# Turning q with DMA transposes of 16-bit halves, and taking the words apart on ScalarE, in a fused attention and feed-forward kernel

## The chip, the cores and the metric

The kernel runs on one core of one Trainium2 chip. The metric is the device time in microseconds (us) of that core for one launch. Every kernel was timed several times beside the kernel before on the same chip. A ratio below is the mean time of one kernel's fast runs over the mean of the other's fast runs of the same rounds, so it is not quite the ratio of the medians quoted beside it.

The names of the profile: PE is TensorE (matmuls), PEld its weight loads, ACT ScalarE, DVE VectorE, POOL GpSimd, SP SyncE. SyncE issues most DMAs; SPq marks its queue.

## The reference, cut to what matters

```python
kv  = einsum('bhsd,bhse->bhde', k, v)     # batch 8, heads 8, seq 576, head_dim 64
out = einsum('bhsd,bhde->bhse', q, kv)
out = out / sqrt(mean(out*out, -1) + 1e-6) * g_norm
x   = out.transpose(0, 2, 1, 3).reshape(4608, 512)
result = (((x @ w1) * (x @ w2)) @ w3) @ w_out
```

In this kernel the matmuls of `q @ kv` take q with head_dim on the partitions, while it arrives with tokens there. It has to be turned: 128x128 blocks of fp32.

## The kernel before

w3 and w_out are folded into one matrix first. Then the work goes by batches: the gates `(x @ w1) * (x @ w2)` of one batch in four parts p (Winograd-style, seven products each), its projection, and in between, in small pieces, the attention of the next batch. TensorE's list is in the program's order; the lists of ScalarE, VectorE and SyncE are ordered by a scheduler when the kernel is built.

```python
def q_t(r):                                   # q of one pair of heads
    q_sb = loaded["q", b, r]
    qt_ps = bank(ps_at, "at").rearrange("p (e i t) -> p e i t", e=2, i=2)
    for e in range(2):
        for i in range(2):
            nc.tensor.transpose(qt_ps[:, e, i, :], q_sb[:, e, i * P:(i + 1) * P], ident)
    qT[r] = work.tile([P, 2, 2, P], FP32, name="qT")
    nc.scalar.copy(qT[r], qt_ps)
...
# winograd: the start of the seven products of a gate
r1 = product("a11", "b11"); p1 = keep("p1", r1)      # keep = ScalarE copy PSUM -> SBUF
r2 = product("s1", "t1");   p5 = keep("p5", r2)
product("s2", "t2", r1);    u2 = keep("u2", r1)      # adds into bank r1: waits for the copy p1
between()                                            # a piece of attention
product("s4", "b22", r2)                             # waits for the copy p5
done("c12", r2, u2)
product("s3", "t3", r1);    u3 = keep("u3", r1)      # waits for the copy u2
...
```

q is called in program order as `begin_q(0, 1)` in piece 0 of the next batch and `begin_q(2, 3)` in piece 2; their users, the products of attention, are in pieces 1 and 5.

Of the kernel before, what the change touches and what calls it, by code (L numbers as in the profile page):

```python
# [10 lines left out]

FP32 = mybir.dt.float32
U32 = mybir.dt.uint32
I64 = mybir.dt.int64
AF = mybir.ActivationFunctionType
ALU = mybir.AluOpType
# [4 lines left out]
def kernel(  # L21
# [32 lines left out]
    nc = tc.nc  # L54
    PSUM = bass.MemoryType.PSUM
    P = 128
# [4 lines left out]
    NP = H // 2  # L61
# [11 lines left out]
    work = ctx.enter_context(tc.tile_pool(name="work", bufs=2))  # L73
    ps_mm = ctx.enter_context(tc.tile_pool(name="ps_mm", bufs=5, space=PSUM))
    ps_at = ctx.enter_context(tc.tile_pool(name="ps_at", bufs=3, space=PSUM))
# [5 lines left out]
    def bank(pool, tag):  # L81
        return pool.tile([P, 512], FP32, name=tag, tag=tag)


    loaded = {}
    q_left = {}
# [43 lines left out]
    def conversion(n, dst, raw, cols=slice(0, 1024)):  # L130

        dst, raw = (t if len(t.shape) == 3 else t[:, cols] for t in (dst, raw))
        if raw.dtype == FP32:
            yield
            nc.vector.tensor_copy(out=dst, in_=raw)
            return
        words = raw.bitcast(U32).rearrange("p (n w) -> p n w", w=2)
        lo, hi = words[:, :, 0], words[:, :, 1]

        low = ab[n % 2][:, NF // 2:].rearrange("p a i t -> p (a i t)")[:, cols]  # L140
        low_bits = low.bitcast(U32)
        if len(dst.shape) == 3:
# [3 lines left out]
            )  # L146
        dst_bits = dst.bitcast(U32)
        nc.scalar.activation(low, lo, AF.Copy, scale=2.0 ** -51, bias=2.0)
# [85 lines left out]
    def all_of(steps):  # L234
        for _ in steps:
            pass


    ident = const.tile([P, P], FP32, name="ident")
# [13 lines left out]
    def keep_warm(n):  # L253

        t = bank(ps_mm, "mm")
        for _ in range(n):
            nc.tensor.matmul(t[:, 0:P], lhsT=ident, rhs=ident, start=True, stop=True)


    def attention(b):  # L260
        kv_b = kv_sb[b % 3]
        qT = {}
# [28 lines left out]
        def q_t(r):  # L291
# [6 lines that stand above are left out]
            qT[r] = work.tile([P, 2, 2, P], FP32, name="qT")  # L298
            nc.scalar.copy(qT[r], qt_ps)

        st = {}

        def q_t_left():
            st["qT"] = work.tile([P, NP, P], FP32, name="qT_left", bufs=1)
            qt_ps = bank(ps_at, "at").rearrange("p (r t) -> p r t", r=NP)
            for r in range(NP):
                nc.tensor.transpose(qt_ps[:, r, :], q_left[b // 2][:, 2 * r:2 * r + 2, :], ident)  # L307
            nc.scalar.copy(st["qT"], qt_ps)

        def norm(o_ps, dsts):  # L310

# [85 lines left out]
        def load_ahead(names, r):  # L397

            if r + 2 < NP:
                load_pair(names, b, r + 2)  # L400
            elif b + 1 < B:
                load_pair(names, b + 1, r + 2 - NP)
                if r + 1 == NP and "k" in names:
                    load_kv_left(b + 1)

        def begin_kv(*rs):
            kv(rs)
            for r in rs:
                load_ahead("kv", r)

        def begin_q(*rs):
            for r in rs:
                q_t(r)
                load_ahead("q", r)

        def begin(r):
            begin_kv(r)
            begin_q(r)

        def finish(h):  # L420
            all_of(product(h))

        return SimpleNamespace(**{f.__name__: f for f in (
            start, begin_kv, begin_q, begin, product, finish, turn, q_t_left, product_left, turn_left,
        )})

    batches = {}

    def batch(b):
        if b not in batches:  # L430
            batches[b] = attention(b)
        return batches[b]

    def steps(b):


        a = batch(b)
        a.start()
        more = b + 1 < B
        fs = [[] for _ in range(8)]  # L440
        if b == 1:
            fs[0].append((a.begin_kv, 0, 1))
        fs[0].append((a.begin_q, 0, 1))
        fs[1] += [(a.begin_kv, 2, 3), (a.finish, 0)]
        fs[2].append((a.begin_q, 2, 3))
        fs[3] += [(a.turn, 0), (a.turn, 1)]
        if more:
            fs[5].append((batch(b + 1).begin_kv, 0, 1))
        fs[5].append((a.finish, 1))
        fs[7] += [(a.turn, 2), (a.turn, 3)]  # L450
        if b % 2:
            fs[2].insert(0, (a.q_t_left,))
            fs[6].append((a.product_left,))
            fs[7].append((a.turn_left,))
            if more:
                fs[7].append((load_q_left, b + 1))
        elif more:
            fs[0].append((load_q_left, b + 1))
        return iter([lambda s=s: [f(*args) for f, *args in s] for s in fs])
# [95 lines left out]
    def run(*step_lists):  # L555

        for steps in zip(*step_lists):
            for step in steps:
                step()
# [50 lines left out]
    def sum_ab(p):  # L610
        aa[p] = {f"a{i + 1}{j + 1}": ab[j][:, p, i, :] for i in range(2) for j in range(2)}
        return sums(aa[p], free["ab", p])
# [10 lines left out]
    def gates(T, p, between, ready=lambda name: None):  # L623
        def done(name, one, two):
            multiply(name, one, two)
            ready(name)

        def multiply(name, one, two):

            dst = ab[int(name[1]) - 1][:, p, int(name[2]) - 1, :]  # L630
            if two is None:
                c = late_pool.tile([P, N], FP32, name="c21")
                nc.scalar.copy(c, one[:, 0, :])  # L633
                nc.vector.tensor_mul(dst, c, one[:, 1, :])
                return
            c = late_pool.tile([P, 2, N], FP32, name="c")
            nc.vector.tensor_add(c, one, two)  # L637
            nc.vector.tensor_mul(dst, c[:, 0, :], c[:, 1, :])  # L638

        winograd(  # L640
            lambda name, w, c: wa[p][name][:, w, c, :],
            lambda name, c: xb[T][name][:, c, :],
            NP // 2, done, between,
        )
# [31 lines left out]
    def stage_tile():  # L676
        return late_pool.tile([P, 3, 2, P], FP32, name="stage")
# [43 lines left out]
    def sum_inner(n, between=lambda: None):  # L721

        s1, s2, s4 = ab_sums
        x = [ab[0][:, :, 0], s1, s2, s4, ab[0][:, :, 1], ab[1][:, :, 0], ab[1][:, :, 1]][n]
        a11, a12, a21, a22 = (
            x[:, 2 * j:2 * j + 2, i * P:(i + 1) * P] for i in range(2) for j in range(2)
        )
        s1, s2, s4 = inner_sums[n % 3]
        nc.vector.tensor_add(s1, a21, a22)
        nc.vector.tensor_sub(s2, s1, a11)  # L730
        nc.vector.tensor_sub(s4, a12, s2)
        between()
        nc.vector.tensor_sub(a21, a11, a21)
        inner[n] = [a11, a12, a22, s1, s2, s4, a21]
# [145 lines left out]
    with tc.manual_schedule(  # L880
# [6 lines left out]
        for e in range(2):  # L887
            nc.scalar.dma_start(
                out=g_row[:, e * D:(e + 1) * D], in_=g_norm.rearrange("(o d) -> o d", o=1)
# [75 lines left out]
    groups = [*range(B - 1), B, B - 1]  # L965
    for n, T in enumerate(groups):
        pieces = steps(T + 1) if n + 2 < NG else iter([])

        def between():
            next(pieces, lambda: None)()  # L970

        for p in range(NF):
            if T and p + 1 == NF:
                sum_1, sum_2, sum_4, sum_3 = sum_ab(p)
                following = {
                    "c12": [], "c22": [sum_1],
                    "c11": [
                        lambda: sum_inner(0, lambda: all_of(f() for f in (sum_2, sum_3))),
                        lambda: sum_inner(1),
                    ],  # L980
                    "c21": [sum_4],
                }
                gates(T, p, between, lambda name: all_of(f() for f in following[name]))
                continue
            gates(T, p, between if T or p else lambda: None)
            if T == 0:
                if p + 1 < NF:
                    run(sum_w(p + 1))
                for _ in range(2):
                    if len(converted) < len(todo):  # L990
                        begin_next()
                        end_next()
                if p + 1 == NF:
                    allocate_projection()
                    run(*(f(i) for i in range(NF) for f in (sum_ab, combine_w3o)))
            else:
                run(sum_ab(p))
        last = n + 1 == NG
        if T:
            project_twice(T, last, [] if last else combine_x(groups[n + 1]))  # L1000
            continue
        project(T, between)
        run(combine_x(1))
        prepare_b()
        for _ in range(3):
            load_b()
        stage = stage_tile()
        inner_sums.append([stage[:, i] for i in range(3)])
# [30 lines left out]
```

## Time and profile before

| | before |
|---|---|
| time | 794.4 us (794.05 to 794.71) |
| TensorE busy | 784.4 of 792.2 us, 99% |
| ScalarE busy | 282.2 us, 36% |
| mean granted TensorE clock | 0.999 |
| turning q on TensorE | 128 + 16 transposes, 17.2 + 2.4 us of busy time |

The first rows say that TensorE sets the time, and that the change takes work off the engine that counts. The records of these transposes overlap (one lasts 275 ns, and 128 of them make 17.2 us, 134 ns each). The clock row matters later: the clock column of the kernel before is 1.00 until behind its last matmul (0:785 and 785:790 us). The lines themselves are in the prediction.

### The profile page before, as it was taken

How to read it: one execution, taken by the hardware profiler on the slowest of the kernel's cores; microseconds unless marked ns; L12 is line 12 of the kernel's file. 1: busy time of each engine (PE TensorE's matmuls, PEld its weight loads, DVE VectorE, ACT ScalarE, POOL GpSimd, SP SyncE). 2: the span in 40 equal slices, each digit the busy share in tenths (PEclk: the TensorE clock that was granted, in tenths of full speed). 3: DMA queues.
4: the chain of work that ended last, by engine and by line, in shares of the span. 5: the costliest groups of instructions: out<-in, count | busy, mean ns of one | idle time of the engine just before them, and what ended most of it. 6: DMA issues, size and time to landing. Idle time of an engine off the chain costs nothing.

```text
span 792.2 us, 14634 instructions
## 1 busy us (share of the span) xinstructions
PE 784.4 (99%) x6003; PEld 683.1 (86%) x6003; DVE 499.0 (63%) x1050; ACT 282.2 (36%) x540; POOL 24.8 (3%) x36
## 2 busy tenths in 40 slices
PE   8999999999999999999999999999999999999998
PEld 5455788888899889988998899889988998899897
DVE  7968999425575558555755576457645765485366
ACT  6677643223332433233323332333233322222221
POOL 0010003410000000000000000000000000000000
PEclk9999999999999999999999999999999999999999
DMA  9996653574138412841284119411810180055015
GB/s 321 339 334 178 190 148 127 191 265 157 54 99 305 110 54 84 298 120 54 88 297 129 54 56 314 130 54 67 307 34 2 60 308 12 1 191 189 1 34 186
DMA packets 72582, 117.60 MB, mean 148 GB/s; under 512 B 16452, under 2 KB 60484, under 8 KB 72516
## 3 DMA queue, kind: packets, MB, share of 16 engines
q1 hardware_dynamic: 70064, 101.86, 40.2%
q10 hardware_dynamic: 2452, 14.81, 5.4%
q8 instruction: 47, 0.77, 0.4%
q14 instruction: 19, 0.16, 0.1%
HBM read 100.27 MB, written 16.38 MB: 147 GB/s over the span
## 4 chain that ended last, share of the span: by engine, by line
PE 96%; DMA 3%; ACT 1%; DVE 0%; SPq 0%; issue 0%; DVEq 0%; ACTq 0%
PE mm L499 58%; PE mm L771 22%; PE mm L481 6%; PE at L278 3%; PE at L348 2%; PE at L297 2%; PE at L381 2%; DMA raw<-in_moe_w_dram 2%; DMA raw<-in_moe_w_out_dram 1%; PE at L468 1%; PE mm L823 0%; PE at L366 0%; PE at L390 0%; PE at L307 0%; DVE inv L317 0%; ACT w_sb L149 0%
## 5 line engine op out<-in xcount | busy, mean ns | idle before, releaser
L499 PE MATMUL mm<-xT,w_sb 128*128 128x256 f32 x768 | 176.2, 379 | 0.0
L499 PEld LDWEIGHTS mm<-xT,w_sb 128*128 128x128 f32 x768 | 145.5, 190 | 20.0 <-issue 0.5
L499 PE MATMUL mm<-xc,ws 128*128 128x256 f32 x576 | 130.4, 379 | 0.0
L499 PEld LDWEIGHTS mm<-xc,ws 128*128 128x128 f32 x576 | 109.4, 190 | 15.2 <-ACT p L512 0.3
L637 DVE TENSOR_TENSOR c<-mm,u 128x512 f32<-128x512 f32 x36 | 24.9, 690 | 153.6 <-PE mm L499 153.4
L512 ACT COPY u<-mm 128x512 f32<-128x512 f32 x74 | 43.3, 585 | 146.5 <-PE mm L499 141.9
L512 ACT COPY p<-mm 128x512 f32<-128x512 f32 x74 | 43.3, 585 | 88.0 <-PE mm L499 85.5
L499 PE MATMUL mm<-xc,w_sb 128*128 128x256 f32 x288 | 69.6, 385 | 0.0
L771 PE MATMUL mm<-w3o_sb,raw 128*128 128x128 f32 x500 | 62.2, 275 | 0.0
L481 PE MATMUL mm<-chunks,ab 128*128 128x512 f32 x128 | 60.2, 601 | 1.6 <-ACT chunks L149 1.0
L499 PE MATMUL mm<-xT,ws 128*128 128x256 f32 x256 | 60.9, 381 | 0.4 <-ACT p L512 0.4
L771 PEld LDWEIGHTS mm<-w3o_sb,raw 128*128 128x128 f32 x500 | 59.0, 192 | 0.2
L499 PEld LDWEIGHTS mm<-xc,w_sb 128*128 128x128 f32 x288 | 52.5, 190 | 7.3 <-ACT u L512 0.3
L499 PEld LDWEIGHTS mm<-xT,ws 128*128 128x128 f32 x256 | 47.2, 190 | 6.7 <-ACT p L512 0.8
L638 DVE TENSOR_TENSOR ab<-c 128x256 f32<-128x256 f32 x108 | 46.7, 433 | 3.1
L637 DVE TENSOR_TENSOR c<-p,u 128x512 f32<-128x512 f32 x36 | 24.9, 691 | 35.5 <-ACT u L512 35.5
L771 PE MATMUL mm<-w3o_sb,ab 128*128 128x128 f32 x336 | 43.7, 275 | 0.0
L782 ACT COPY u<-mm 128x512 f32<-128x512 f32 x23 | 13.5, 585 | 83.9 <-DVE raw L795 43.4
L317 DVE TENSOR_REDUCE inv<-sq 128x8 f32<-128x512 f32 (+1 forms) x40 | 23.4, 627 | 31.6 <-ACT sq L316 31.6
L481 PEld LDWEIGHTS mm<-chunks,ab 128*128 128x128 f32 x128 | 21.9, 190 | 22.6 <-issue 15.8
L771 PEld LDWEIGHTS mm<-w3o_sb,ab 128*128 128x128 f32 x336 | 41.0, 192 | 0.3
L633 ACT COPY c<-mm 128x256 f32<-128x256 f32 x36 | 13.4, 372 | 48.4 <-PE mm L499 48.4
(150 smaller groups left out, 1109.9 us busy)
## 6 DMA issues: line engine op xcount, KB each, us to landing
w3o_sb<-w3o_l SPq DMA_DIRECT2D x26, 896.0 KB, 5.3
raw<-in_moe_w_dram SPq DMA_DIRECT2D x31, 512.0 KB, 7.4
raw<-w3o_l SPq DMA_DIRECT2D x13, 896.0 KB, 4.6
w3o_sb<-w3o_l ACTq DMA_DIRECT2D x11, 896.0 KB, 4.6
k_sb<-in_k_dram SPq DMA_DIRECT2D x32, 256.0 KB, 3.9
v_sb<-in_v_dram SPq DMA_DIRECT2D x32, 256.0 KB, 4.6
q_sb<-in_q_dram SPq DMA_DIRECT2D x32, 256.0 KB, 4.1
out_dram<-raw SPq DMA_DIRECT2D x14, 512.0 KB, 5.1
```

The costliest lines, as they stand in the source:

```text
L278: nc.tensor.matmul(kv_ps[e * D:(e + 1) * D, r - rs[0], :], lhsT=k_sb[:, e, cols] if j < J else kl[:, 2 * r + e, :], rhs=v_sb[:, e, cols] i ...
L297: nc.tensor.transpose(qt_ps[:, e, i, :], q_sb[:, e, i * P:(i + 1) * P], ident)
L317: nc.vector.tensor_reduce(out=inv[:, i], in_=sq.rearrange("p (h d) -> p h d", d=D), axis=AX.X, op=ALU.add)
L348: nc.tensor.matmul(o_ps[l][tokens, n * D:(n + 1) * D], lhsT=qT[r][rows, e, i, tokens], rhs=kv_b[rows, e, r, :], start=True, stop=True,)
L381: nc.tensor.transpose(t_ps[:, j, :], st[r // 2][:, j // 2, j % 2, m:m + 2, :], ident)
L481: nc.tensor.matmul(sums_ps[half][m], lhsT=w3T[half, c][:, m, :], rhs=chunks[:, c, 1, :], start=(c == 0), stop=(c == KF - 1),)
L499: nc.tensor.matmul(ps[:, u, :], lhsT=lhsT(a_name, u, c), rhs=rhs(b_name, c),  start=(u == 0 and c == 0 and to is None), stop=(c == chunks ...
L512: nc.scalar.copy(t, ps)
L637: nc.vector.tensor_add(c, one, two)
L638: nc.vector.tensor_mul(dst, c[:, 0, :], c[:, 1, :])
L771: nc.tensor.matmul(to[:, i, :], lhsT=x[:, c, :], rhs=y[:, c, :], start=new and place // 4 not in seen, stop=(c == 1), skip_group_check=True,)
L782: nc.scalar.copy(t[:, 0:4], ps[0])
```

## The change

The intent: free TensorE of the q transposes of batches 1 to 7. The DMA transposes are used on 16-bit elements, so each fp32 word is taken apart into two 16-bit planes (first copy, ScalarE), the planes are transposed by DMA from one SBUF tile to another, and the words are put together again (second copy, ScalarE). To give this chain time, q of heads 0 to 3 of the next batch moves from piece 0 into piece 6 of the batch before. Below, a pair is what one call `begin_q(0, 1)` or `begin_q(2, 3)` turns: two q tiles, eight blocks of 128x128. The four blocks of left-over tokens that are turned together are called a left-over block.

```diff
+    def turn_by_dma(dst, src):
+        def words(t):
+            return t.bitcast(U16).rearrange("p (n w) -> p n w", w=2)
+        def planes(t):
+            return t.bitcast(U16).rearrange("p (w n) -> p w n", w=2)
+        nc.scalar.copy(planes(dst), words(src).rearrange("p n w -> p w n"))
+        nc.sync.dma_start_transpose(
+            out=src.bitcast(U16).rearrange("p (a t) -> p a t", t=P), in_=dst.bitcast(U16)
+        )
+        nc.scalar.copy(words(dst), planes(src).rearrange("p w n -> p n w"))
 ...
         def begin_q(*rs):
             for r in rs:
-                q_t(r)
+                q_by_dma(r)
                 load_ahead("q", r)
 ...
-        fs[0].append((a.begin_q, 0, 1))
 ...
+        if more:
+            fs[6].append((batch(b + 1).begin_q, 0, 1))
```

Batch 0 keeps the TensorE transposes. The left-over tokens (`q_t_left`) are turned by DMA as well. Cut: `q_by_dma`, which allocates qT and calls `turn_by_dma`, and a `begin_first` that starts batch 1's q in the first gate.

More of the change, by code (lines that the diff above doesn't have):

```diff
@@ L13 @@
 U32 = mybir.dt.uint32
+U16 = mybir.dt.uint16
 I64 = mybir.dt.int64
@@ L299, in q_t, with q_by_dma @@
             nc.scalar.copy(qT[r], qt_ps)
+        def q_by_dma(r):
+            qT[r] = work.tile([P, 2, 2, P], FP32, name="qT")
+            turn_by_dma(
+                qT[r].rearrange("p e i t -> p (e i t)"), loaded["q", b, r].rearrange("p e n -> p (e n)")
+            )
         st = {}
@@ L304, in q_t_left @@
             st["qT"] = work.tile([P, NP, P], FP32, name="qT_left", bufs=1)
-            qt_ps = bank(ps_at, "at").rearrange("p (r t) -> p r t", r=NP)
-            for r in range(NP):
-                nc.tensor.transpose(qt_ps[:, r, :], q_left[b // 2][:, 2 * r:2 * r + 2, :], ident)
-            nc.scalar.copy(st["qT"], qt_ps)
+            turn_by_dma(
+                st["qT"].rearrange("p r t -> p (r t)"), q_left[b // 2].rearrange("p h d -> p (h d)")
+            )
         def norm(o_ps, dsts):
@@ L417, in begin, with begin_first @@
             begin_kv(r)
-            begin_q(r)
+            q_t(r)
+            load_ahead("q", r)
+        first_done = []
+        def begin_first():
+            if not first_done:
+                first_done.append(begin_q(0, 1))
         def finish(h):
@@ L423, in attention @@
         return SimpleNamespace(**{f.__name__: f for f in (
-            start, begin_kv, begin_q, begin, product, finish, turn, q_t_left, product_left, turn_left,
+            start, begin_kv, begin_q, begin_first, begin, product, finish, turn, q_t_left, product_left, turn_left,
         )})
@@ L984 @@
                 continue
-            gates(T, p, between if T or p else lambda: None)
+            gates(T, p, between if T or p else lambda: batch(1).begin_first())
             if T == 0:
```

## The prediction

> **What bounds the kernel now.** I read the page's first part, then the chain that ended last, then the groups of the lines that the change touches, then the order of time in one steady stretch. Busy time and chain come first:
>
> ```profile
> PE 784.4 (99%) x6003; PEld 683.1 (86%) x6003; DVE 499.0 (63%) x1050; ACT 282.2 (36%) x540; POOL 24.8 (3%) x36
> ...
> PE 96%; DMA 3%; ACT 1%; DVE 0%; SPq 0%; issue 0%; DVEq 0%; ACTq 0%
> ```
>
> TensorE (PE) is busy for 784.4 of 792.2 us and carries 96% of the chain. Time taken off it is time taken off the kernel, as long as nobody makes it wait. ScalarE (ACT) has about 500 us idle in all, so its total cannot bind; its place in time can. The groups concerned (busy us, mean ns, idle before):
>
> ```profile
> L297 PE MATMUL at<-ident,q_sb 128*128 128x128 f32 x128 | 17.2, 275 | 0.0
> L307 PE MATMUL at<-ident,ql_sb 128*128 128x128 f32 x16 | 2.4, 272 | 0.0
> L299 ACT COPY qT<-at 128x512 f32<-128x512 f32 x32 | 17.5, 600 | 0.1
> L308 ACT COPY qT_left<-at 128x512 f32<-128x512 f32 x4 | 2.4, 594 | 0.0
> L148 ACT ACTIVATE ab<-raw 128x1024 f32<-128x1024 uint32 x18 | 21.1, 1170 | 2.4 <-DMA raw<-in_moe_w_out_dram 1.6 <-DVE w_sb L161 0.8
> ```
>
> The q transposes are pipelined: 17.2 us for 128 is 0.134 us each, half the 275 ns that one record lasts. The last line is the nearest relative of the new copies: ScalarE, 1024 elements, reading every second word of SBUF, 1.17 us.
>
> Last, the timeline of the same steady stretch (start, duration, engine, what; the brackets are idle time before):
>
> ```profile
> 260.57 0.37 SPq L94 DMA_DIRECT2D k_sb<-in_k_dram  x1
> ...
> 263.23 0.63 SPq L104 DMA_DIRECT2D vl_sb<-in_v_dram  x1
> ...
> 265.81 3.62 PE L499 MATMUL mm<-xc,ws 128*128 128x256 f32 x16
> 266.01 0.58 ACT L512 COPY p<-mm 128x512 f32<-128x512 f32 x1 [1.15 <-PE mm L499]
> 267.73 0.58 ACT L512 COPY p<-mm 128x512 f32<-128x512 f32 x1 [1.14 <-PE mm L499]
> 269.26 0.60 PE L307 MATMUL at<-ident,ql_sb 128*128 128x128 f32 x4
> 269.51 0.59 ACT L512 COPY u<-mm 128x512 f32<-128x512 f32 x1 [1.20 <-PE mm L499]
> 269.70 1.04 PE L297 MATMUL at<-ident,q_sb 128*128 128x128 f32 x8
> 270.47 1.09 ACT L299 COPY qT<-at 128x512 f32<-128x512 f32 x2
> ```
>
> Here is the weak place. A product of the gate takes about 1.72 us of TensorE (the two p copies start that far apart). TensorE goes on into the same PSUM bank one product later, so a p copy may end at most 1.72 us after its bank is ready; it ends about 0.8 us after. Slack: some 0.9 us. ScalarE's holes between these copies are 1.14 to 1.20 us.
>
> [...]
>
> **The change part by part.** Removed from TensorE: the first batch still turns its q there (16 transposes); 28 pairs of heads in batches 1 to 7 and 4 left-over blocks do not. That is 112 x 0.134 = 15.0 us plus the whole 2.4 us of the ql group, 17.4 us; with the small gaps where weight loads start[...] 17.8 us. All of it lies on the path. Full gain: 794.4 - 17.8 = 776.6, that is 2.2%.
>
> Removed from ScalarE: 28 + 4 PSUM copies, 32 x 0.6 = 19 us. Added: 64 copies of 1024 16-bit values, 64 x 1.05 to 1.17 = 67 to 75 us. Net +48 to +56, ScalarE 282 to about 335 us of 790, 42%. Not a bound.
>
> Added to DMA: 32 transposes of 256 KB, 8.4 MB beside 117.6 MB. [...] From issue to landing I take 3 to 4 us (an estimate: the q loads of the same size land in 2.9 to 8.3, median 4.1), and the second of a pair 1 to 2 us later. HBM traffic does not change.
>
> Moved: q of the next batch is turned one projection earlier, so TensorE's first use of it has tens of us to spare; heads 2 and 3 have about 1.5 gates, some 18 us. So the user of qT should not wait. But the built kernel's order on ScalarE shows where the second copy of each q stands, and it waits for the DMA at the head of ScalarE's list. There are 14 pairs of q's. In six the order is: first copy, two squares, first copy, square root, c, p, p, then both second copies, then u. In six it is: c, second copy, p, second copy, p. One has both second copies ahead of the two p's, and one is in the busy first gate. Placed on the before timeline:
>
> Order one (product ends 262.3): first copies end at 263.4 and 265.5, c at 266.3, p at 266.9 and 268.3, both in time. The transposes can issue only behind the k and v loads, at 263.9 and about 265.6, and land at perhaps 267.5 and 269. Second copies run 268.3 to 270.5, then u to 271.1. TensorE wants u done by 270.8. Loss 0.3 to 0.5 us, more if the DMA is late.
>
> Order two (product ends 291.3 in the same trace): first copies end at 292.4 and 294.6, c at 295.3. The transpose issues at 292.6 and lands between 295.2 and 296.6. Second copy to 296.4 to 297.7, p to 297.0 to 298.3; TensorE wants it at 296.6. Loss 0.5 to 1.8, say 1.2 us, and a little again at the second p.
>
> Sum: 6 x 0.4 + 6 x 1.2 + about 3 for the pair with both copies ahead + 1 in the first gate + 1 for the four left-over blocks = 14.6 us with that DMA; with one that is always in time it would be about 9, from occupation of ScalarE alone. Net: 17.8 less 9 to 14.6, a gain of 3 to 9 us. I put it at 789.0.
>
> **The rivals.** First, the full gain: the copies fit in the holes and TensorE never waits, 777 us. For it: ScalarE is idle 64% of the time and before shows next to no TensorE wait on it. Against: copies of 1.05 to 1.17 us in holes of 1.14 to 1.20 leave nothing. Second, slow transposes: if one lands 6 to 8 us after issue,[...] each pair blocks ScalarE for 3 us more in order two and 2 to 3 in order one: 13 pairs x 2.5 = 32 us, time about 820. For it: the loads just ahead, and DMA slices at 0.91 busy[...]. Third, the transposes hold up SyncE's queue or the w3o stream, and the projection waits for weights: I give it little, since projections come after the q work and streams are loaded three deep; it would cost a few us each, 795 to 800. Fourth, a hidden one: the weights' conversion in the first gate already fills ScalarE, and a blocked copy there costs 2 to 5 us once.
>
> **Range and chances.** Best case 776.6 sets the lower end: faster by over 2% means below 778.5, so all waits together must stay under 2 us; with some 28 insertions on a tight engine I give that 0.11. A moderately slow DMA sets the upper end at 806. Slower by over 2% (above 810.3) needs 33 us of waits, the second rival in full: 0.15. The rest, 0.74, is within 2%.
>
> **What would show it.** Right: TensorE's busy time down by 17 to 18 us to about 767; ScalarE's near 335; new TensorE waits on p and u copies of 8 to 16 us in all; ScalarE waits on the transposing DMA of under 25 us in all; transposes landing in 3 to 5 us. Wrong: TensorE idle under 3 us more (full gain), ScalarE waiting over 40 us for the DMA with landings above 6 us (slow transposes), first copies much longer than 1.2 us, or TensorE waiting for qT or for w3o loads.

What is cut from it are figures that no trace of this case shows: a paragraph of transposing times, DMA bandwidths and copy times, the DMA time and the two clauses of the second rival that used such a bandwidth, and a length of 1.09 us for one pair of q's on TensorE (the trace before has 0.87 to 0.93 us from a pair's first record to the next matmul, as in 413.28 to 414.15). The forecast's sum was 17.8 us gained, less 9 to 14.6 us of waits, so 789.0. The length stood behind the 0.4 us of gaps between 17.4 and 17.8. Of the 1.05 to 1.17 us taken for a copy the upper end is the row quoted above; the lower one was read in no trace then (the first copies of the changed kernel took 1.046 us). HBM traffic is 100.27 MB read and 16.38 MB written in both profiles.

## The result, and the profile after

The changed kernel takes 826.1 us (823.65 to 830.05) against 794.4: ratio 1.0403 (1.0362 to 1.0445), 4% slower. The prediction was 789, range 777 to 806. Its result is correct.

Busy time and the chain that ended last, of the changed kernel:

```profile
PE 784.0 (95%) x5875; PEld 675.1 (82%) x5875; DVE 500.1 (61%) x1050; ACT 330.1 (40%) x572; POOL 28.1 (3%) x36
...
PE 82%; DMA 9%; ACT 4%; POOL 2%; DVE 2%; issue 1%; SPq 0%; DVEq 0%; POOLq 0%; ACTq 0%
```

Two things stand out. TensorE no longer holds 96% of the chain: DMA and ScalarE have come into it. And its busy time has not fallen, although 128 instructions are gone: what remains has become slower. The mean granted clock says so too: 0.983 in place of 0.999.

The groups concerned, changed kernel (busy us, mean ns, then idle time before and what ended it):

```profile
L530 PE MATMUL mm<-xT,w_sb 128*128 128x256 f32 x768 | 178.5, 382 | 9.4 <-ACT u L543 9.4
L530 PE MATMUL mm<-xc,ws 128*128 128x256 f32 x576 | 134.8, 386 | 12.0 <-ACT p L543 12.0
...
L274 ACT COPY qT<-q_sb 128x1024 uint16<-128x1024 uint16 x28 | 32.6, 1165 | 33.1 <-DMA q_sb<-qT 32.8
L270 ACT COPY qT<-q_sb 128x1024 uint16<-128x1024 uint16 x28 | 29.3, 1046 | 1.3 <-PE at L371 1.0
```

The copies cost what was predicted: 1.05 us the first, 1.17 us the second. But ScalarE stands still for 33 us in front of the second copies, waiting for the DMA, and TensorE then stands still in front of its matmuls, waiting for ScalarE's p and u copies. In the list of all waits these sum to 20.8 us (p, seven times) and 9.4 us (u, six times). Before, it was 0.4 us. The lines of that list (us in total, times, longest), first of the kernel before, then of the changed kernel:

```profile
PE mm L499 <- ACT p L512: 0.4, 1, 0.4
```

```profile
PE mm L530 <- ACT p L543: 20.8, 7, 8.8
PE mm L530 <- ACT u L543: 9.4, 6, 2.4
```

One pair in the order that the prediction called order two, changed kernel, in order of time (start, duration):

```profile
306.54 3.67 SPq L271 DMA_TRANSPOSE q_sb<-qT  x2
...
308.69 0.35 ACT L664 COPY c<-mm 128x256 f32<-128x256 f32 x1
...
311.30 1.16 ACT L274 COPY qT<-q_sb 128x1024 uint16<-128x1024 uint16 x1 [2.25 <-DMA q_sb<-qT]
312.36 0.58 ACT L543 COPY p<-mm 128x512 f32<-128x512 f32 x1
...
313.00 1.99 PE L530 MATMUL mm<-xc,ws 128*128 128x256 f32 x8 [2.21 <-ACT p L543]
```

ScalarE is done with c at 309.0. Its next instruction is a second copy, whose transpose was issued at 306.54 and is there only at 311.3. The p copy behind it needs nothing of the DMA, and its bank has long been ready (the product in it ends at 309.06); it starts only at 312.36, behind the second copy. So here ScalarE kept the order of its list, idle for 2.25 us. TensorE needs the bank and loses 2.21 us.

The largest single wait is in the first projection, changed kernel:

```profile
148.14 0.89 POOL L725 TENSOR_TENSOR stage<-w3o_sb,stage 128x256 f32<-128x256 f32 x1
...
149.06 0.32 SPq L729 DMA_DIRECT2D w3o_l<-stage  x1
...
151.66 1.24 SPq L271 DMA_TRANSPOSE q_sb<-qT  x1
...
154.23 0.34 SPq L729 DMA_DIRECT2D w3o_l<-stage  x1
...
154.66 1.30 SPq L271 DMA_TRANSPOSE q_sb<-qT  x1
...
156.68 1.16 ACT L274 COPY qT<-q_sb 128x1024 uint16<-128x1024 uint16 x1 [10.44 <-DMA q_sb<-qT]
...
159.59 1.07 ACT L543 COPY p<-mm 128x512 f32<-128x512 f32 x2
...
160.22 6.28 PE L530 MATMUL mm<-raw 128*128 128x256 f32 x16 [8.79 <-ACT p L543]
```

The first copies of this pair were done at 143.7 and 145.8. But SyncE issues in its own order, and in front of the transposes stood a store that waits for GpSimd (its last subtraction ends at 149.03), and behind that store four k and v loads (149.48 to 151.56). ScalarE stood 10.44 us, TensorE 8.79 us. And look at the last line's duration: 16 records take 6.28 us, where everywhere before they take 3.62 us.

Where the 31.4 us between the two profiled spans (792.2 and 823.6) are:

| part | us | from |
|---|---|---|
| q transposes gone | -14.1 | 14 pairs x 0.88 + 4 blocks x 0.44, measured below |
| TensorE waits for p and u copies | +29.8 | 20.8 + 9.4; before 0.4 |
| slower matmuls at a lowered clock | +8.9 | after the waits of 8.79, 2.17, 2.42 and 2.96 us, 16 records took 6.28, 5.41, 5.41 and 6.72 us, in place of the 3.72 us that they take after the other u waits |
| restart after a wait | +3.5 | an estimate, 13 waits x 0.27: from one attention start to a later one it is 52.83 us (472.63 to 525.46) in place of 51.68; a pair less (0.88) and a wait of 1.76 leave 0.27. Ten of the eleven such stretches from 140 to 610 us give 0.26 to 0.28 |
| launch | +2.4 | first attention matmul at 49.88 in place of 47.49; other runs of these kernels lie at 47.2 to 50.3, so this is spread |
| sum | 30.5 | of 31.4 |

The clock column of the profile would give 12.0 us for the lowered clock. But the clock was already lowered during 5.8 us of the waits (from 155.19 to 160.22 and from 564.79 to 565.51), and that time is in the row of the waits.

### The profile page after: what moved, and what is told of

Same layout as the page of the kernel before. It is cut to its first block, busy times and chain, and to the rows that moved or that the text cites. A ratio compares the mean times of both kernels' runs of the same rounds, so it can differ in the third digit from the quotient of the medians.

```text
span 823.6 us, 14474 instructions
## 1 busy us (share of the span) xinstructions
PE 784.0 (95%) x5875; PEld 675.1 (82%) x5875; DVE 500.1 (61%) x1050; ACT 330.1 (40%) x572; POOL 28.1 (3%) x36
## 3 DMA queue, kind: packets, MB, share of 16 engines
HBM read 100.27 MB, written 16.38 MB: 142 GB/s over the span
## 4 chain that ended last, share of the span: by engine, by line
PE 82%; DMA 9%; ACT 4%; POOL 2%; DVE 2%; issue 1%; SPq 0%; DVEq 0%; POOLq 0%; ACTq 0%
PE mm L530 47%; PE mm L802 20%; PE mm L512 7%; DMA q_sb<-qT 6%; PE at L295 2%; PE at L371 2%; ACT qT L274 2%; PE at L404 2%; DMA w3o_l<-stage 2%; DMA w3o_sb<-w3o_l 1%; PE at L499 1%; ACT qT L270 1%; POOL stage L723 1%; DMA raw<-in_moe_w_out_dram 1%; POOL stage L725 1%
## 5 line engine op out<-in xcount | busy, mean ns | idle before, releaser
L530 PE MATMUL mm<-xT,w_sb 128*128 128x256 f32 x768 | 178.5, 382 | 9.4 <-ACT u L543 9.4
L530 PE MATMUL mm<-xc,ws 128*128 128x256 f32 x576 | 134.8, 386 | 12.0 <-ACT p L543 12.0
L668 DVE TENSOR_TENSOR c<-mm,u 128x512 f32<-128x512 f32 x36 | 24.8, 689 | 153.6 <-PE mm L530 130.8
L530 PE MATMUL mm<-xT,ws 128*128 128x256 f32 x256 | 62.7, 389 | 0.0
L530 PEld LDWEIGHTS mm<-xT,ws 128*128 128x128 f32 x256 | 49.7, 196 | 7.9 <-ACT p L543 0.4
L274 ACT COPY qT<-q_sb 128x1024 uint16<-128x1024 uint16 x28 | 32.6, 1165 | 33.1 <-DMA q_sb<-qT 32.8
```

Of the source, the lines that this page charges most:

```text
L274: nc.scalar.copy(words(dst), planes(src).rearrange("p w n -> p n w"))
L530: nc.tensor.matmul(ps[:, u, :], lhsT=lhsT(a_name, u, c), rhs=rhs(b_name, c),  start=(u == 0 and c == 0 and to is None), stop=(c == chunks ...
L668: nc.vector.tensor_add(c, one, two)
```

## The experiments

The theories. W: the second copies, at the head of ScalarE's list, wait for a transpose to land, and what stands behind them holds up TensorE. O: the 64 extra copies simply occupy ScalarE where it has no room. Q, a part of W: the long wait comes from SyncE's list. C: after a wait TensorE runs at a lowered clock. Then there is the question whether transposing by DMA is slow in itself.

### Second copies on GpSimd

```diff
-        nc.scalar.copy(words(dst), planes(src).rearrange("p w n -> p n w"))
+        nc.gpsimd.tensor_copy(out=words(dst), in_=planes(src).rearrange("p w n -> p n w"))
```

> Second copies (those that wait for the transpose) go to GpSimd, which is idle 97% of the time; first copies stay on ScalarE; same DMAs. Theory W (the wait in ScalarE's list is what costs): TensorE waits on p and u copies fall from 30 us to under 5, the clock returns to 0.998 or more, time 777 to 786. Rival O (occupation of ScalarE by 64 extra copies is what costs): half the copies remain, so about half the loss, 800 to 808. Rival D (landing too late for the user of qT): TensorE would now wait for qT itself, and the time stays above 810.

785.4 us, ratio 0.9888 (0.9866 to 0.9909): 41 us faster than the changed kernel, and faster than the kernel before. The clock is 0.997. The copies, in the groups of this run by shape:

```profile
L274 POOL COPY qT<-q_sb 128x1024 uint16<-128x1024 uint16 x28 | 38.5, 1393 | 432.0 <-DMA q_sb<-qT 335.3 <-ACT p L543 69.8 <-ACT xT L406 24.5
```

GpSimd stands 335 us in front of them for the DMA, and no wait of TensorE in this run's list is put down to these copies. TensorE's waits on p and u copies fall to 3.0 us. But the edit takes away two things from ScalarE, the waits and half of the occupation.

### First copies on GpSimd

The missing corner: the edit is the same for the other copy. ScalarE keeps 32 extra copies, as in the run above, but now those that wait.

```diff
-        nc.scalar.copy(planes(dst), words(src).rearrange("p n w -> p w n"))
+        nc.gpsimd.tensor_copy(out=planes(dst), in_=words(src).rearrange("p n w -> p w n"))
```

> The fourth corner of two by two: first copies on GpSimd, second copies, which wait for the transpose, stay on ScalarE. ScalarE's extra occupation is as in the run with second copies on GpSimd (785 us, 32 copies), its waits as in the changed kernel. Theory W (the wait of the second copy): TensorE still waits 20 us or more on p and u copies, the clock stays under 0.995, time 808 to 826. Rival O (occupation): like the other half, 784 to 792. If both halves matter alike: about 800 to 806.

824.1 us, ratio 1.0380 (1.0365 to 1.0396); clock 0.985. The groups of this run:

```profile
L530 PE MATMUL mm<-xT,w_sb 128*128 128x256 f32 x768 | 176.8, 380 | 6.2 <-ACT u L543 6.2
L530 PE MATMUL mm<-xc,ws 128*128 128x256 f32 x576 | 135.0, 386 | 13.0 <-ACT p L543 13.0
...
L530 PE MATMUL mm<-raw 128*128 128x256 f32 x32 | 8.8, 436 | 14.6 <-ACT p L543 14.6
```

TensorE waits 33.8 us on p and u copies. Of this, 14.6 us is one wait in the first projection that the edit makes longer: GpSimd comes to the first copies of that pair only at 156.89, after its w3o subtractions. The other waits, 19.2 us, are nearly those of the changed kernel without its longest (21.4), though ScalarE has 32 copies fewer. With the same number of copies on ScalarE, it is 785 when the waiting ones are elsewhere and 824 when they are not. Occupation cannot be the main cause; the waits are. Theory O falls. No run left the second copies on ScalarE and moved them further back in its list, so whether a later place there would do as well stays open.

### Both copies on GpSimd

The two edits above together.

> First and second copies on GpSimd; ScalarE gets nothing extra. A GpSimd copy of this shape took 1.15 us where second copies ran there. If ScalarE's first copies still cost TensorE something (Rival O in its mild form), 780 to 783; if not, as with second copies alone, 784 to 787; if GpSimd's two copies in series bring q too late or disturb VectorE, above 790.

786.9 us, ratio 0.9896 (0.9873 to 0.9919). The first copies on ScalarE cost nothing that shows here: freeing it of them as well gains nothing over 785.4.

### Second copies on VectorE

```diff
-        nc.scalar.copy(words(dst), planes(src).rearrange("p w n -> p n w"))
+        nc.vector.tensor_copy(out=words(dst), in_=planes(src).rearrange("p w n -> p n w"))
```

> Second copies on VectorE, 64% busy, first copies on ScalarE. If what matters is only that the wait leaves ScalarE, as good as GpSimd: 784 to 788. If any engine that TensorE's loop depends on must not wait for a transpose in the middle of its list, VectorE now idles on the DMA some 20 to 35 us in all and part of that reaches TensorE through the c sums: 790 to 805.

787.7 us, ratio 0.9919 (0.9899 to 0.994). VectorE now idles 37.1 us for these DMAs (31.2 and 5.9), as ScalarE did, and yet TensorE waits only 4.5 us for it, once. So the first of the two expectations came true. An explanation, which no run here tests, is that VectorE mostly has more slack than the wait: in the changed kernel it idles 153.6 us in front of its 36 sums `c<-mm,u`, 130.8 of them waiting for TensorE.

### No DMA at all

Wrong result: the transpose is left out, and the second copy reads q.

```diff
-        nc.sync.dma_start_transpose(
-            out=src.bitcast(U16).rearrange("p (a t) -> p a t", t=P), in_=dst.bitcast(U16)
-        )
-        nc.scalar.copy(words(dst), planes(src).rearrange("p w n -> p n w"))
+        nc.scalar.copy(words(dst), words(src))
```

> Wrong result on purpose: the transposing DMA is left out, the second copy reads q straight from its tile; both copies stay on ScalarE. Theory W: without a DMA to wait for, ScalarE's occupation alone costs little: 780 to 790, TensorE waits on ScalarE under 8 us. Rival O: TensorE still waits 15 us or more on p and u copies and the time stays above 800.

795.4 us, ratio 1.0010 (0.9990 to 1.0029), above the range of W and below that of O. The group that waits:

```profile
L527 PE MATMUL mm<-xc,ws 128*128 128x256 f32 x576 | 133.4, 381 | 9.5 <-ACT p L540 9.5
```

The waits are twelve of 0.8 us each. The scheduler, with no DMA to allow for, sets all four copies of a pair in front of the p copies, so this is occupation in a worse place than in the changed kernel. It shows that occupation is not free, as the prediction said (about 9), and that even without any wait for a DMA the change would have gained nothing in that order.

### A plain DMA in place of the transpose

Wrong result. ScalarE's list is the same, instruction for instruction.

```diff
-        nc.sync.dma_start_transpose(
-            out=src.bitcast(U16).rearrange("p (a t) -> p a t", t=P), in_=dst.bitcast(U16)
-        )
+        nc.sync.dma_start(out=src.bitcast(U16), in_=dst.bitcast(U16))
```

> Wrong result on purpose: a plain DMA copy of the same 256 KB from the same tile to the same tile stands in for each transpose. If the transposing itself is slow, the plain copies issue in about 0.4 us each instead of 1.24 to 1.5, land in about 3 us instead of 4.2, and the time falls to 800 to 815. If the loads ahead in the same queue set the landing, it lands in 4 us or more as well and the time stays at 820 to 830.

816.8 us, ratio 1.0274 (1.0252 to 1.0296). The DMA issues by kind, first of the changed kernel, then of this run (times issued, KB each where known, median us to landing):

```profile
q_sb<-qT SPq DMA_TRANSPOSE x28, 4.3
...
ql_sb<-qT_left SPq DMA_TRANSPOSE x4, 3.0
```

```profile
q_sb<-qT SPq DMA_DIRECT2D x28, 256.0 KB, 4.6
ql_sb<-qT_left SPq DMA_DIRECT2D x4, 256.0 KB, 2.3
```

The time lies between the two expectations, so by time alone it is undecided. The landing decides one thing: a plain copy of the pairs lands no sooner (4.6 us) than the transpose (4.3). For the left-over blocks, in front of which no k and v loads are queued, the transpose takes 3.0 and the plain copy 2.3 us. So some 0.7 us is the transposing (a transpose took 1.24 us or more of SyncE's time to issue, the two plain copies read at 151.51 and 154.51 in this run 0.47 us), and the step from 3.0 to 4.3 goes with the company of loads; that these loads are its cause was argued from this, not tried by itself. The 4.3 is a median over both transposes of a pair: after the first gate the first one, behind the loads, landed after 4.2 to 6.7 us, the second after 3.1 to 4.3, where the trace tells it. The gain of 9 us comes with a shorter wait in the first projection (5.4 us in place of 8.8) and a clock of 0.990.

### The early stage on TensorE again

```diff
         def q_by_dma(r):
+            if b == 1 or (b == 2 and r < 2):
+                return q_t(r)
```

and the left-over blocks of batches 1 and 3 likewise.

> Undoes the change only around the first projection: batch 1, the first half of batch 2 and the first two left-over blocks are turned on TensorE again; the 11 later pairs and ScalarE's order there are as in the changed kernel. Theory W (second copies at the head of ScalarE's list wait for a transpose to land; the longest such wait, 10.4 us, comes from a transpose that stands in SyncE's list behind stores that wait for GpSimd): the 8.8 us TensorE wait near 151 us goes, with it the lowered clock of the next 20 us (some 5 us) and one 1.4 us wait; the restored transposes cost about 4.5 us. 826 becomes about 815; the 2.2 and 1.3 us waits of the later pairs stay. Rival S (the early stage is not special, the loss is spread evenly over 14 pairs): 11 of 14 pairs remain, so about 819 to 820, with a TensorE wait over 5 us still somewhere.

816.2 us, ratio 1.0267 (1.0235 to 1.0300). The 8.8 us wait is gone; the largest on a p or u copy is now 3.9 us. The time is where W has it, but S is only 3 us away and the runs spread from 812.4 to 818.3, so this run alone does not decide.

### The stores issued by GpSimd

The same question without touching q: the three kinds of w3o stores leave SyncE's list (three like edits, shown as one). ScalarE's list is the same.

```diff
 def prepare_b():
-                nc.sync.dma_start(          # w3o_l2[7], w3o_l2[n] blocks, w3o_l2[n] stages
+                nc.gpsimd.dma_start(
```

> The changed kernel with the w3o stores of the first projection issued by GpSimd and no longer by SyncE; ScalarE's order is the same instruction for instruction. Theory Q (the 8.8 us wait came from a transpose that stood in SyncE's list behind stores waiting for GpSimd): that wait falls to 3 us or less, the clock between 140 and 180 us returns to 1.0, time 811 to 817. Rival (the transpose is slow there by itself): wait and time as in the changed kernel, 823 to 830.

812.9 us, ratio 1.0216 (1.0194 to 1.0238), 13 us less than the changed kernel. The place of the long wait, in this run's order of time:

```profile
141.22 6.35 SPq L271 DMA_TRANSPOSE q_sb<-qT  x2
...
148.72 2.21 ACT L274 COPY qT<-q_sb 128x1024 uint16<-128x1024 uint16 x2 [4.99 <-DMA q_sb<-qT]
...
151.47 5.41 PE L530 MATMUL mm<-raw 128*128 128x256 f32 x16 [2.54 <-ACT p L543]
```

The first transpose is issued at 141.22, right behind its first copy, in place of 8 us later, and the wait falls from 8.79 to 2.54 us. Theory Q holds. It is the issue that came sooner, not the landing: that transpose, behind four k and v loads, still took 7.4 us to land. The clock in this stretch did not quite return: 0.96 between 140 and 180 us, and 16 records still take 5.41 us after the wait.

### TensorE's waits filled with idle work

Unused matmuls of the identity fill the waits; ScalarE's list is the same, instruction for instruction.

```diff
+    def fill(n):
+        t = bank(ps_at, "at")
+        for _ in range(n):
+            nc.tensor.matmul(t[:, 0:P], lhsT=ident, rhs=ident, start=True, stop=True)
 ...
         p5 = keep("p5", r2)
+        if fills[0]:
+            fill(fills[0])          # 8 in gate part 3, 32 in the first projection
         product("s2", "t2", r1)
 ...
         done("c12", r2, u2)
+        if fills[1]:
+            fill(fills[1])          # 5 in gate part 1
         product("s3", "t3", r1)
```

> The changed kernel with idle-time filler on TensorE: unused 128x128 matmuls of the identity stand where it waits (8 before the second half of every fourth gate, 5 in every second gate, 32 in the first projection: sized a little under the waits of 2.2, 1.3 to 1.6 and 8.8 us). ScalarE's order is the same instruction for instruction. The waits stay in length, only filled. Theory C (the matmuls after a wait run at a lowered clock because TensorE stood still, and this is the second part of the loss, 0.983 against 0.999 of 824 us, some 11 us): granted clock back to 0.995 or more, matmuls after the waits at their usual 3.6 us per 16 records, time 812 to 818. Rival F (the lower clock has nothing to do with the waits, or costs nothing on the path): clock stays near 0.983 and the time at 824 to 832.

818.8 us (814.9 to 821.1), just above the expected 812 to 818; ratio 1.0287 (1.0251 to 1.0323), against 1.0403 without the filling. Two stretches of the changed kernel, then the same of this run (window, length, then busy time of PE, PEld, DVE, ACT and POOL with counts, granted clock, DMA share, GB/s):

```profile
380.00:400.00 20.00, 17.83 (x170) 15.01 (x168) 8.62 (x17) 9.54 (x17) 0.00 (x0) 0.94 0.41 104
560.00:580.00 20.00, 17.04 (x77) 14.42 (x76) 9.54 (x23) 6.81 (x12) 0.00 (x0) 0.83 0.34 56
```

```profile
380.00:400.00 20.00, 19.91 (x196) 17.55 (x195) 10.60 (x22) 9.96 (x18) 0.00 (x0) 1.00 0.40 107
560.00:580.00 20.00, 20.00 (x166) 19.54 (x165) 17.64 (x46) 5.57 (x11) 0.00 (x0) 1.00 0.50 172
```

The clock column goes from 0.94 and 0.83 to 1.00, and over the whole run from 0.983 to 0.999. So the lowered clock comes from standing still, and it costs: the ratio falls by 0.0116, some 9 us of 794 (the two intervals leave 5 to 14). Expected were some 11 us from the clock column; the slower matmuls of the changed kernel, 8.9 us in the table above, fit better.

Which waits were followed by it can be read from the changed kernel's trace. Its clock column is 0.50 from 155.19 to 165.43 us, from 397.54 to 400.95, from 455.56 to 458.98 and from 564.79 to 571.62, once at the start (11.83 to 15.25, after a wait of 2.66 us), and 1.00 in the rest up to 823. The first four belong to TensorE's waits of 8.79, 2.17, 2.42 and 2.96 us on p and u copies: 0.50 begins within the wait or up to 1.3 us after its end. After the last of these, 8 records that otherwise take 1.99 us took 3.78 us. The other nine waits on p and u copies, of 0.63 to 2.32 us, were not followed by it. So length alone does not decide: after the wait of 2.17 us 8 records took 3.25 us, after one of 2.21 us the usual 1.99. What decides between such waits no run here was made to show.

### Both edits: early stage on TensorE, second copies on GpSimd

> Two edits at once, aimed at the best version: batch 1, the first half of batch 2 and two left-over blocks on TensorE, all other second copies on GpSimd. If the early stage costs GpSimd's version anything (it lost about 2 us to before by 184 us), this gains it back less what the transposes cost: 781 to 785. If a pair of q's on TensorE costs 1.09 us, undoing three pairs and two blocks costs 4.5 us and the time is 785 to 789.

783.8 us (783.67 to 785.46), ratio 0.9857 (0.9838 to 0.9876), 1.4% faster than the kernel before, correct, clock 0.999: the best version here. It also measures what turning a pair on TensorE is worth. The attention of one batch starts twice, with one pair of q's turned in between; the two starts in the kernel before, then in this run:

```profile
340.48 0.69 PE L278 MATMUL at<-v_sb,k_sb 128*64 128x64 f32 x16
...
369.01 0.39 PE L278 MATMUL at<-v_sb,k_sb 128*64 128x64 f32 x6
```

```profile
337.20 0.69 PE L295 MATMUL at<-v_sb,k_sb 128*64 128x64 f32 x16
...
364.85 0.34 PE L295 MATMUL at<-v_sb,k_sb 128*64 128x64 f32 x4
```

28.53 us between the starts before, 27.65 without the pair: 0.88 us, 0.11 us for each of the eight transposes, of which one record lasts 275 ns; it is not the 1.09 us of the second expectation. Where a left-over block lies in the stretch as well, it is 28.97 against 27.65 with the block by DMA too, so the block is worth 0.44 us. For the whole change that is 14 x 0.88 + 4 x 0.44 = 14.1 us, and by this measure 794.4 - 14.1 = 780.3 us would have been the best case: 1.8%, within the 2%. This version turns 11 pairs and 2 blocks by DMA, 11 x 0.88 + 2 x 0.44 = 10.6 us, and gained 11.0 us on the medians of its rounds (794.84 and 783.82). Nothing is left to find in the part that it does move.

## Why the prediction was wrong, point by point

The prediction had the mechanism, ScalarE's in-order wait in front of the p and u copies, and the two orders. Its sum failed, and it lacked one term.

- **"Full gain: 794.4 - 17.8."** Mis-sized: the term is 14.1 us. It took busy time of pipelined transposes for the path, and for a pair a length (1.09 us) that the trace before does not show. So, by this measure, "faster by over 2%" was not to be had at all.
- **"Sum: 6 x 0.4 + 6 x 1.2 + about 3 ... = 14.6 us."** Mis-sized: 30.2 us in the profiled run. The six u waits are about 1.6 us each on average and the p waits, without the longest, 2.0 us, in place of 0.4 and 1.2. The step beneath is "from issue to landing I take 3 to 4 us": the median of the pairs is 4.3, and the first transpose of a pair, on which ScalarE waits first, took 4.2 to 6.7 us after the first gate (4.68 in the pair shown above). The time was the author's estimate, beside the q loads of the kernel before (2.9 to 8.3 us, median 4.1); the transposes of the pairs, behind k and v loads, took longer (4.3), and so did plain copies there (4.6).
- **"The transposes can issue only behind the k and v loads."** Right for the later pairs. For the first projection it was not asked what else stands in SyncE's list: a store that waits for GpSimd. With the stores moved, 2.54 of the 8.79 us remain, so it made 6.3 us of them. The third rival looked at that queue the wrong way round: it asked whom the transposes hold up, and not who holds up the transposes.
- **The missing term.** No step of the sum asked what TensorE's clock does after a wait. It costs 8.9 us by the records after the four waits and about 9 us by the filling. In part for the same reason the sign "TensorE's busy time down ... to about 767" failed: it stayed at 784.0.
- **"Slow transposes"**, the second rival, named about 820 us, near the result, but with landings of 6 to 8 us for each pair; of the landings that the trace tells, only three are above 6 us (8.7, 6.2 and 6.7). So the nearness is luck. The time came from smaller waits, one queue and the clock.
- **"Occupation of ScalarE alone ... about 9."** The run without a DMA shows 9.5 us of waits, in another order of ScalarE's list, so the agreement is partly luck; ScalarE with first copies alone shows next to nothing.
- Right: the durations of the copies (1.05 and 1.17), ScalarE's total (330.1 against 335), and that the user of qT never waits: with the second copies on GpSimd, which came later still, TensorE shows no wait for qT.

## What to carry to other kernels

Here a copy that waited for a DMA held up what stood behind it in ScalarE's list (2.21 us of TensorE in the pair shown). So put such an instruction on an engine behind which nobody waits, even a slower one: the copy took 1.17 us on average on ScalarE and 1.39 us on GpSimd, and yet the kernel was 41 us longer with it on ScalarE. Before adding a DMA to a queue, ask what stands in front of it there and what that waits for. Where TensorE bounds, a wait can count twice, once for itself and once for slower matmuls behind it: here the four of 2.17, 2.42, 2.96 and 8.79 us did (8.9 us of slower matmuls), the nine others, of 0.63 to 2.32 us, did not.
